# First six chunks' decays as sums of logarithms on TensorE, an explicit order of all tasks, and fillers on an on-chip tile

## The chip, the cores and the metric

One core of one Trainium2 chip runs the whole program. The metric is the device time of one execution in microseconds (us); lower is better. Engines: PE is TensorE (PEld its weight loads), DVE is VectorE, ACT is ScalarE, POOL is GpSimd, SP issues the DMAs.

## What is computed

Gated linear attention with a decay per channel, and behind it an RWKV channel mix. B=4, H=8, S=768, D=48; the mix has d_model 384 and d_ff 1024.

```python
f = 1 / (1 + exp(-f_logit))
for t in range(S):                       # per batch and head
    state = f[t][:, None] * state + outer(k[t], v[t])
    x[t] = q[t] @ state
x_prev = x shifted by one step
xk = mu_k * x + (1 - mu_k) * x_prev ;  xr = mu_r * x + (1 - mu_r) * x_prev
out = sigmoid(xr @ w_r) * (relu(xk @ w_k) ** 2 @ w_v)
```

The weights w_k, w_r, w_v come as 64-bit words.

## The kernel before

The sequence is cut into 24 chunks of 128 steps (6 for each batch entry) and into 8 units of three chunks. A chunk holds all eight heads as four pairs, 128 channels by 4x128 steps.

**Attention of chunk i** (`add_attention`). SP loads qk{i}, v{i} and, for a unit, the gate logits f{u}; ScalarE takes their sigmoid (`sf`, L469, L475). `b`: VectorE's scan multiplies the gates up along time into PSUM (L293). `ln`, `rb`: ScalarE makes 1/b as exp(-ln b) (L299, L301). `q`: q times b (L303); `kr`: GpSimd's k times 1/b (L311, L312); `n`, `k`: one Newton step for that reciprocal on VectorE (L323; L315, L319), which leaves k with its sign turned. `TR`: four TensorE transposes of k (L363); `kt`: their copy. `SP`: scores (L378) and state sums (L398). `m` masks the scores (for chunk 0 by ScalarE and GpSimd), `g`, `za`, `zb`, `T` carry the state. `YA`, `YB`: outputs from the state and from the chunk itself (L415), with `w` between them; `y` copies them to x (L447, scale -1).

**The mix of unit u** (`add_mix`). When y of its three chunks is there, six small DMAs spread rows of x (`sp`, L505). Then `d`, `xm` (L517 or L527; L530, L535), a split into a high part `xh` (L543, L544) and a low part `xl` (L550, GpSimd), and the products on TensorE, all at L558: 8 times `F` (9 matmuls each, with w_k), 3 times `R` (9 each, w_r), 6 times `W` (12 each, w_v): 171 matmuls of 128x384 for a unit. Between F and W stand relu `r`, squares `h` and `kk`, and their difference `l` (L596, GpSimd).

**Weights** (`add_words`). 18 pieces (4 of w_r, 8 of w_k, 6 of w_v) are loaded as words and turned into two parts each: `S`, `T`, `X` on VectorE (L676, L685, L688), `H` on ScalarE (L691), `L` on GpSimd (L695). F{u}.f needs piece f of w_k, R all of w_r, W{u}.t0 pieces 0 to 2 of w_v and W{u}.t1 pieces 3 to 5. Later 15 checks `cm` read the words once more (L745).

**Order.** `Plan.schedule` lists the tasks one after the other: among those that are ready it takes the one that starts earliest by its own estimates, with the table `PLACE` to decide between near ones; `emit` pins that order on every engine, so each engine works strictly down its list. A task with two ways (say `l` on GpSimd or VectorE) takes the one that would be done first. Where the list has TensorE waiting before the first F, fillers (L753: 128x64 matmuls of the loaded identity, in fours, not before 14 us and not before `cst` has landed) are put in. ScalarE begins with the sigmoid table, and `ex` (L768) changes to the table of exp and ln after the gates of units 0 and 1; the gates of unit 2 change there and back (L475, L477).

Of the kernel before, what the change touches and what calls it, by code (L numbers as in the profile page):

```python
# [111 lines left out]

class Plan:

    def __init__(self):
# [879 lines left out]
```

## Time and profile before

| | |
|---|---|
| three runs | median 353.2 us (352.62 to 354.17) |
| profiled execution | 352.86 us, span of the trace 350.7 us |
| busy | PE 318.9, DVE 248.7, ACT 213.3, POOL 195.1 us |
| first and last matmul of a mix | 50.82 us, 345.06 us |
| unit 0's first F to unit 1's first F | 50.82 to 92.29 us |

In the trace times count from the start of the span. A row of the timeline has start, duration, engine, line, operation, what is written and read, and in brackets the idle time before it with what ended it. "L558 PE" is all of the mix's matmuls.

### The profile page before, as it was taken

What the parts mean: (1) busy time and instruction counts of PE and PEld (TensorE: products, weight loads), DVE (VectorE), ACT (ScalarE), POOL (GpSimd) and SP (SyncE); (2) the same over time, 40 slices, a digit from 0 to 9 for tenths busy, and PEclk for the clock granted to TensorE, in tenths of its full rate; (3) what the DMA queues carried; (4) which work ended last, traced back from release to release, by engine and by line L of the source; (5) the groups of instructions that cost most, each with busy time, mean ns of one, the idle gap of its engine ahead of it and who ended that gap; (6) DMA issues with size and microseconds to landing.
All of it is one profiled execution on the core that took longest, in us unless ns stands there. A gap on an engine that the chain in (4) does not pass through costs nothing.

```text
span 350.7 us, 10802 instructions
## 1 busy us (share of the span) xinstructions
PE 318.9 (91%) x4450; PEld 304.2 (87%) x4450; DVE 248.7 (71%) x489; ACT 213.3 (61%) x437; POOL 195.1 (56%) x235
## 2 busy tenths in 40 slices
PE   0078799899999999999999999999999999999993
PEld 0067589788999999999999999999999999999993
DVE  7987899989989699758975689549963943913110
ACT  2785678777686818873686558582876156705520
POOL 2554588987687177715784268526880634814400
PEclk9998859999999999999999999999999999999999
DMA  8999252335741674638323352042401100010001
GB/s 270 406 359 377 88 195 97 120 105 178 242 126 38 223 251 123 218 117 286 124 83 121 118 194 86 3 122 68 137 10 41 48 27 19 1 47 22 1 26 52
DMA packets 20650, 45.32 MB, mean 129 GB/s; under 512 B 2928, under 2 KB 13040, under 8 KB 20592
## 3 DMA queue, kind: packets, MB, share of 16 engines
q1 hardware_dynamic: 20592, 44.55, 38.3%
q8 instruction: 37, 0.61, 0.7%
q14 instruction: 21, 0.17, 0.2%
HBM read 38.64 MB, written 4.72 MB: 124 GB/s over the span
## 4 chain that ended last, share of the span: by engine, by line
PE 78%; POOL 6%; DVE 4%; DMA 3%; ACT 3%; issue 3%; SPq 1%; DVEq 0%; POOLq 0%
PE pm L558 61%; PE py L415 7%; PE pss L378 3%; PE pm L363 3%; DMA f<-in_zt 2%; PE pss L398 2%; POOL k2l L596 2%; POOL wv L695 2%; POOL wk L695 1%; DMA words<-in_wv 1%; PE py L753 1%; DVE xm L535 1%; DVE qk L319 1%; POOL qk L311 0%; SPq L682 0%
## 5 line engine op out<-in xcount | busy, mean ns | idle before, releaser
L558 PE MATMUL pm<-xh,wk 128*128 128x384 f32 x384 | 105.3, 345 | 1.1 <-POOL wk L695 1.0
L558 PE MATMUL pm<-wv,k2h 128*128 128x384 f32 x384 | 98.9, 338 | 0.3 <-POOL wv L695 0.3
L596 POOL TENSOR_TENSOR k2l<-kk,k2h 128x384 fp32r<-128x384 f32 x64 | 68.3, 1069 | 36.5 <-DVE kk L588 25.3
L550 POOL TENSOR_TENSOR xl<-xm,xh 128x384 fp32r<-128x384 f32 x48 | 50.1, 1053 | 49.8 <-DVE xh L544 24.6
L558 PEld LDWEIGHTS pm<-xh,wk 128*128 128x128 f32 x384 | 70.1, 189 | 3.3 <-POOL wk L695 1.9
L558 PEld LDWEIGHTS pm<-wv,k2h 128*128 128x128 f32 x384 | 68.8, 188 | 0.8 <-POOL wv L695 0.6
L558 PE MATMUL pm<-xl,wk 128*128 128x384 f32 x192 | 64.8, 337 | 0.0
L558 PE MATMUL pm<-wv,k2l 128*128 128x384 f32 x192 | 64.5, 336 | 0.0
L581 ACT ACTIVATE r<-pm 128x384 f32<-128x384 f32 x56 | 27.5, 491 | 25.1 <-PE pm L558 23.7
L558 PE MATMUL pm<-wr,xh 128*128 128x384 f32 x144 | 37.9, 345 | 0.4 <-DVE kk L588 0.4
L586 ACT ACTIVATE k2h<-r 128x384 fp32r<-128x384 f32 x64 | 33.5, 525 | 5.6 <-DVE r L582 3.6
L648 DVE TENSOR_TENSOR o<-pm,lg 128x384 f32<-128x384 f32 x24 | 13.3, 553 | 33.0 <-PE pm L558 33.0
L558 PEld LDWEIGHTS pm<-xl,wk 128*128 128x128 f32 x192 | 36.4, 189 | 0.0
L558 PEld LDWEIGHTS pm<-wv,k2l 128*128 128x128 f32 x192 | 36.1, 188 | 0.0
L363 PE MATMUL pm<-ident,qk 128*128 128x128 f32 x96 | 17.1, 307 | 20.4 <-DVE qk L319 19.8
L588 DVE SCALAR_TENSOR_TENSOR kk<-pm,r 128x384 f32<-128x384 f32 x34 | 18.9, 555 | 22.4 <-ACT r L581 21.6
L293 DVE TENSOR_TENSOR_SCAN pm<-f,low 128x512 f32<-128x512 f32 x24 | 33.7, 1404 | 0.3 <-ACT ktk L367 0.2
L447 ACT ACTIVATE x<-py 64x128 f32<-64x128 f32 (+1 forms) x69 | 21.4, 310 | 19.9 <-PE py L415 18.2
L363 PEld LDWEIGHTS pm<-ident,qk 128*128 128x128 f32 x96 | 12.5, 154 | 21.9 <-DVE qk L319 19.6
L415 PEld LDWEIGHTS py<-qk,z 64*64 64x64 f32 x704 | 17.0, 141 | 11.9 <-issue 5.2
L415 PE MATMUL py<-qk,z 64*64 64x64 f32 x704 | 23.4, 236 | 4.0 <-ACT stage L447 1.4
L535 DVE SCALAR_TENSOR_TENSOR xm<-pm,mu_sb,x 128x384 f32<-128x384 f32 x42 | 25.7, 612 | 0.7
(102 smaller groups left out, 570.9 us busy)
## 6 DMA issues: line engine op xcount, KB each, us to landing
qk<-in_qkt SPq DMA_DIRECT2D x24, 512.0 KB, 4.3
words<-in_wv SPq DMA_DIRECT2D x12, 512.0 KB, 4.3
f<-in_zt SPq DMA_DIRECT2D x7, 768.0 KB, 6.4
v<-in_vt SPq DMA_DIRECT2D x24, 192.0 KB, 3.3
out<-o SPq DMA_DIRECT2D x24, 192.0 KB, 2.4
words<-in_wk SPq DMA_DIRECT2D x6, 512.0 KB, 4.6
words_k2h<-in_wk SPq DMA_DIRECT2D x4, 384.0 KB, 6.0
words_k2l<-in_wk SPq DMA_DIRECT2D x4, 384.0 KB, 8.4
```

The costliest lines, as they stand in the source:

```text
L293: pl.add(f"b{i}", ga, ("V", 1.25, 1, lambda: nc.vector.tensor_tensor_scan(b().rearrange(FL), f().rearrange(FL), self.low.rearrange(FL), 1. ...
L363: nc.tensor.transpose(pk()[:, j], k()[:, j], self.ident)
L415: first[c, h] = nc.tensor.matmul(to, lhs, rhs, start=(c, h) not in first, stop=stop, skip_group_check=True)
L447: e.activation(o, i_, AF.Copy, scale=-1.0)
L535: pl.add(f"xm{u}.{n}{j}", pr, ("V", 0.62, 0, lambda xm=xm, n=n, j=j: nc.vector.scalar_tensor_tensor(xm(), pm("d", u, j)[:, :UT], self.mu_s ...
L550: e.tensor_tensor(lo(), xm(), hi().bitcast(F32), op=ALU.subtract)
L558: nc.tensor.matmul(ps, lhs(a, j), rhs(bb, j), start=ends[0] and i == 0, stop=ends[1] and i == len(pr) - 1)
L581: pl.add(f"r{u}.{f}", kf, ("A", 0.5, 0, lambda r=r, ps=ps: nc.scalar.activation(r(), ps(), AF.Relu)), ("V", 0.56, 0, lambda r=r, ps=ps: nc ...
L586: pl.add(f"h{u}.{f}", kf, ("A", 0.53, 0, lambda r=r, hi=hi: nc.scalar.activation(hi(), r(), AF.Square)), after=[f"r{u}.{f}"], **kw)
L588: pl.add(f"kk{u}.{f}", kf, ("V", 0.56, 0, lambda r=r, ps=ps, kk=kk: nc.vector.scalar_tensor_tensor(kk(), ps(), 0.0, r(), op0=ALU.max, op1= ...
L596: e.tensor_tensor(lo(), kk(), hi().bitcast(F32), op=ALU.subtract)
L648: pl.add(f"o{u}.{t}", kv, ("V", 0.56, 0, lambda t=t, ps=ps, o=o: nc.vector.tensor_tensor(o(), ps(), lg()[:, t], op=ALU.mult)), after=[f"W{ ...
```

## The change

- For chunks 0 to 5 (`early`, units 0 and 1) the decays are made another way. VectorE clamps the gate logits in place (`sf`, now a maximum with a per-partition bound); TensorE transposes them (`zT`, 4 transposes), ScalarE takes exp and ln(1+.) of the transposes (`ez`, `ln`), TensorE multiplies with a triangle of ones (`b`, 4 matmuls of 128x128), which gives the sums of logarithms along time, and ScalarE's `rb` and `e` take exp of plus and minus that sum. The scan, `n`, `k` and `g` of these chunks are gone, and so is the sigmoid of units 0 and 1; y's sign is +1 there, and za multiplies with bl of the chunk before.
- ScalarE begins with the table of exp and ln; `ex` is gone. The triangle is one more load (`tri`).
- `ORDER` names every task in turn, and the engine where there are two; `schedule` follows it. Of 112 tasks `l` and `xl`, all on GpSimd before, 32 stand on VectorE.
- A filler is one matmul of 256 columns on `low`, a tile that a memset makes; it may come from 3.6 us on. There are 10 of them (20 before). `py` is cleared whole.

```diff
-FILL = (14.0, 0.85)
+FILL = (3.6, 0.9)
...
-PLACE = {
-    "cst": 0.45, "ex": 7.598, "c0": 0.906, "cm0": -1.376, "c2": -1.069, "v0": -3.667, "b0": 0.122, "bl0": -1.422, "rb0": 0.016,
...
+ORDER = """
+wr2 wrS2 f0.0 wrT2 sf0.0 wrX2 wr3 cst f0.1 wv0 tri f1 zT0 wrS3 wrT3 wrH2 sf0.1 wrX3 wvS0 wvT0 wvX0 sf1 ez0 ln0 zT1 wrH3 ez1
...
+        given = [t.partition(":")[::2] for t in reversed(ORDER.split())]
...
+            if given:
+                n, e = given.pop()
...
+        if early:
+            def sums_of_logs():
+                for j in range(NP):
+                    nc.tensor.matmul(b()[:, j], f()[:, j], self.tri, start=True, stop=True)
...
+            def over_time():
+                for j in range(NP):
+                    nc.tensor.transpose(zt()[:, j], f()[:, j], self.ident)
...
+            pl.add(f"ez{i}", ga, ("A", 0.63, 0, lambda: nc.scalar.activation(f(), zt(), AF.Exp, scale=-1.0)),
+                   uses=[("pm", ("z", i))])
+            pl.add(f"ln{i}", ga, ("A", 0.63, 0, lambda: nc.scalar.activation(f(), f(), AF.Ln, bias=1.0)), after=I("ez"))
...
+            pl.add(f"rb{i}", ga, ("A", 0.63, 0, lambda: nc.scalar.activation(rb(), b(), AF.Exp)),
+                   takes=[("rb", i)], uses=[("pm", ("b", i))])
+            pl.add(f"e{i}", ga, ("A", 0.63, 0, lambda: nc.scalar.activation(b(), b(), AF.Exp, scale=-1.0)),
...
-            pl.add(f"g{i}", ga, ("G", 0.25, 0, lambda: gate(nc.gpsimd)),
+            if not early:
+                pl.add(f"g{i}", ga, ("G", 0.25, 0, lambda: gate(nc.gpsimd)),
...
+        def sure(cs=slice(0, UC)):
+            nc.vector.tensor_scalar(t(cs), t(cs), self.sure, None, op0=ALU.max)
...
-            self.nc.tensor.matmul(self.py[:, 0, 256:320], self.ident, self.ident[:, :64], start=False, stop=True, skip_group_check=True)
+            self.nc.tensor.matmul(self.py[:, 0, 256:], self.low[:, 0], self.low[:, 1:3], start=False, stop=True, skip_group_check=True)
...
-    nc.scalar.preload_act_table_set(SIGMOID_SET)
+    nc.scalar.preload_act_table_set(EXP_SET)
...
-    nc.vector.memset(k.py[:, :, :320], 0.0)
+    nc.vector.memset(k.py[:, :, :], 0.0)
```

How the order moves, at the head of three engines. First VectorE before, just behind the pieces of w_r (pm are PSUM buffers, f the gates, low the scan's lower bound, bl the last column of b, rb its reciprocal):

```order
L688 SCALAR_TENSOR_TENSOR lg0_119<-lg0_119,pm3_94 128x288
L293 SCALAR_TENSOR_TENSOR pm0_91<-f0_61,low_78 128x512
L297 COPY bl_80<-pm0_91 128x4
L293 SCALAR_TENSOR_TENSOR pm1_92<-f0_61,low_78 128x512
L297 COPY bl_80<-pm1_92 128x4
L293 SCALAR_TENSOR_TENSOR pm2_93<-f0_61,low_78 128x512
L303 TENSOR_TENSOR qk1_65<-qk1_65,pm1_92 128x512
L293 SCALAR_TENSOR_TENSOR pm3_94<-f1_62,low_78 128x512
```

And VectorE in the change, from the first clamp on (L517 is the clamp; L730, L739, L742 are S, T, X of a piece of weights, x0 and lg0 of w_r, words0 of w_v, words_k2h of w_k; L350 is q):

```order
L517 TENSOR_SCALAR f0_61<-f0_61,sure_70 128x512
L742 SCALAR_TENSOR_TENSOR x0_106<-x0_106,pm2_95 128x288
L730 TENSOR_SCALAR pm3_96<-words0_122 128x512
L739 SCALAR_TENSOR_TENSOR pm3_96<-words0_122,pm3_96 128x512
L742 SCALAR_TENSOR_TENSOR words0_122<-words0_122,pm3_96 128x512
L517 TENSOR_SCALAR f1_62<-f1_62,sure_70 128x1536
L350 TENSOR_TENSOR qk0_64<-qk0_64,pm2_95 128x512
L348 COPY bl_82<-pm2_95 128x4
L730 TENSOR_SCALAR pm2_95<-words_k2h0_131 128x384
L739 SCALAR_TENSOR_TENSOR pm2_95<-words_k2h0_131,pm2_95 128x384
```

The scans are gone from VectorE's list, and pieces of w_v and w_k stand in their place. TensorE before, its first rows (L363 transposes k, L378 and L398 are SP, L753 a filler, L415 an output):

```order
L363 MATMUL pm0_91<-ident_68,qk0_64 128x128 x4
L363 MATMUL pm1_92<-ident_68,qk1_65 128x128 x4
L378 MATMUL pss_87<-qk0_64 64x64 x16
L398 MATMUL pss_87<-v0_101,ktk0_99 48x48 x16
L753 MATMUL py_88<-ident_68 128x64 x4
L415 MATMUL py_88<-qk0_64,z01_73 64x64 x4
```

And in the change (L807 is a filler, L327 zT, L321 b, L413 TR):

```order
L807 MATMUL py_90<-low_80 128x256
L327 MATMUL pm1_94<-ident_68,f0_61 128x128 x4
L807 MATMUL py_90<-low_80 128x256
L327 MATMUL pm0_93<-ident_68,f0_61 128x128 x4
L321 MATMUL pm2_95<-tri_69,f0_61 128x128 x4
L321 MATMUL pm1_94<-tri_69,f0_61 128x128 x4
L327 MATMUL pm0_93<-ident_68,f1_62 128x128 x4
L327 MATMUL pm3_96<-ident_68,f1_62 128x128 x4
L807 MATMUL py_90<-low_80 128x256 x2
L413 MATMUL pm0_93<-ident_68,qk0_64 128x128 x4
```

Fillers and the gates' transposes and sums stand ahead of the first TR now. ScalarE before, from its first sigmoid of unit 1 on (L299 and L301 are ln and rb):

```order
L475 ACTIVATE f1_62<-f1_62 128x1536
L768 ACT_TABLE_LOAD
L299 ACTIVATE rb0_95<-pm0_91 128x512
L301 ACTIVATE rb0_95<-rb0_95 128x512
L299 ACTIVATE rb1_96<-pm1_92 128x512
L301 ACTIVATE rb1_96<-rb1_96 128x512
```

And in the change (L330 ez, L332 ln, L334 rb, L336 e):

```order
L330 ACTIVATE f0_61<-pm1_94 128x512
L332 ACTIVATE f0_61<-f0_61 128x512
L745 CAST wr0_85<-x0_106 128x288
L330 ACTIVATE f0_61<-pm0_93 128x512
L332 ACTIVATE f0_61<-f0_61 128x512
L334 ACTIVATE rb0_97<-pm2_95 128x512
L336 ACTIVATE pm2_95<-pm2_95 128x512
```

The table change between gates and ln is gone, and a chunk has four passes of 128x512 where it had two beside its sigmoid.

## Rows read from the trace of the kernel before

**Rows 1.** The page's second part: PE's busy tenths in 40 slices of the span.

```profile
PE   0078799899999999999999999999999999999993
```

**Rows 2.** Stretches: start:end, length, then busy us (and count) of each engine.

```profile
0.00:50.80 50.80, 26.42 (x712) 23.16 (x712) 43.06 (x92) 32.73 (x65) 26.03 (x44) 0.88 0.80 284
50.80:92.30 41.50, 39.85 (x384) 36.60 (x381) 37.97 (x68) 30.31 (x65) 34.55 (x35) 0.98 0.47 147
92.30:131.20 38.90, 38.90 (x637) 37.51 (x636) 33.13 (x61) 25.34 (x53) 24.34 (x31) 1.00 0.52 162
```

**Rows 3.** The chain that ended last, its start: start, us, what.

```profile
5.05 7.82 DMA f<-in_zt
12.89 1.48 ACT f L475
14.39 1.28 ACT L768
```

**Rows 4.** The same chain: the first F's of units 2 and 3.

```profile
131.42 3.13 PE pm L558 x18
...
168.96 3.18 PE pm L558 x18
```

**Rows 5.** Timeline of TensorE from 110 to 115 us: one chunk's steps between matmuls of R.

```profile
110.16 0.60 PE L363 MATMUL pm<-ident,qk 128*128 128x128 f32 x4
110.52 0.60 PE L558 MATMUL pm<-wr,xh 128*128 128x384 f32 x2
...
112.26 0.46 PE L415 MATMUL py<-qk,z 64*64 64x64 f32 x16
112.54 0.65 PE L378 MATMUL pss<-qk 64*64 64x64 f32 x32
...
114.17 0.62 PE L558 MATMUL pm<-wr,xh 128*128 128x384 f32 x2
```

**Rows 6.** VectorE's groups from 0 to 92.3 us: count | busy us, mean ns.

```profile
L293 DVE TENSOR_TENSOR_SCAN pm<-f,low 128x512 f32<-128x512 f32 x9 | 12.0, 1337 | 0.1
L323 DVE TENSOR_TENSOR pm<-rb,pm 128x512 f32<-128x512 f32 x8 | 5.5, 691 | 0.3 <-ACT rb L301 0.3
L319 DVE SCALAR_TENSOR_TENSOR qk<-pm,qk 128x128 f32<-128x128 f32 x16 | 3.8, 281 | 0.0
L315 DVE SCALAR_TENSOR_TENSOR qk<-pm,qk 128x256 f32<-128x256 f32 x8 | 3.3, 418 | 0.7 <-DVE pm L323 0.5
L685 DVE SCALAR_TENSOR_TENSOR pm<-words,pm 128x512 int32<-128x512 int32 x6 | 4.2, 692 | 0.1
L685 DVE SCALAR_TENSOR_TENSOR pm<-words_k2h,pm 128x384 int32<-128x384 int32 x4 | 2.2, 562 | 0.1
L544 DVE CAST xh<-xm 128x384 fp32r<-128x384 f32 x5 | 1.9, 390 | 0.2
```

**Rows 7.** ScalarE's passes of 128x512 over the whole span: count | busy us, mean ns.

```profile
L301 ACT ACTIVATE rb<-rb 128x512 f32<-128x512 f32 x24 | 15.0, 626 | 0.4
```

**Rows 8.** Timeline, the end of unit 0's y (ACT) to its first F.

```profile
37.48 0.98 ACT L447 ACTIVATE x<-py 128x256 f32<-128x256 f32 x3 [1.15 <-PE py L415]
...
50.82 0.69 PE L558 MATMUL pm<-xh,wk 128*128 128x384 f32 x1
```

**Rows 9.** Timeline of TensorE: the same filler at two places.

```profile
45.97 1.81 PE L753 MATMUL py<-ident 128*128 128x64 f32 x8
54.69 1.00 PE L753 MATMUL py<-ident 128*128 128x64 f32 x8
```

**Rows 10.** GpSimd's groups from 50.8 to 92.3 us.

```profile
L695 POOL TENSOR_TENSOR wv<-words,wv 128x512 fp32r<-128x512 f32 x6 | 9.9, 1643 | 1.5 <-ACT wv L691 1.5
L695 POOL TENSOR_TENSOR wk<-words_k2l,wk 128x384 fp32r<-128x384 f32 x4 | 4.2, 1046 | 1.1 <-ACT wk L691 1.1
```

**Rows 11.** Timeline, two scans, the first with GpSimd at work beside it.

```profile
12.19 1.57 DVE L293 TENSOR_TENSOR_SCAN pm<-f,low 128x512 f32<-128x512 f32 x1
14.41 1.23 DVE L293 TENSOR_TENSOR_SCAN pm<-f,low 128x512 f32<-128x512 f32 x1
```

More of the change, by code (lines that the diff above doesn't have):

```diff
@@ L27 @@
 NF = DFF // P
-SIGMOID_SET = "sigmoid_and_others"
 EXP_SET = "natural_log_exp_and_others"
@@ L31 @@
 N, U = B * NCH, B * NU
+NL = 2
+SURE, FULL = -44.0, 40.0
 NQ, NFB = 4, 3
@@ L160, in schedule @@
         order = []
+        given = [t.partition(":")[::2] for t in reversed(ORDER.split())]
         while ready:
             best = None
-            for n, names in ready.items():
+            if given:
+                n, e = given.pop()
+                _, _, ways, _, takes, _ = self.tasks[n]
+                way = next(w for w in ways if w[0] == e or not e)
+                at = max([0.0] + [min(slots[b[0]])[0] for b in takes]
+                         + [end[m] for m in ready[n] if way_of[m] != way[0]])
+                best = None, n, max(at, free[way[0]]), way
+            for n, names in ready.items() if best is None else ():
                 _, place, ways, _, takes, _ = self.tasks[n]
@@ L180, in schedule @@
             e, us, port, _ = way
-            if e == "P" and self.filler and "cst" in end:
-                t = max(free["P"], read, FILL[0], end["cst"])
-                stop = t + (start - t - 0.25) * FILL[1]
+            if e == "P" and self.filler:
+                t = max(free["P"], read, FILL[0])
+                stop = t + (start - t - 0.15) * FILL[1]
                 cold = t + 6.0 if last_p == "F" else 0.0
-                while t + (us4 := 1.76 if t < cold else 0.88) < stop:
+                while t + (us4 := 0.9 if t < cold else 0.46) < stop:
                     name = f"fill{len(order)}"
-                    fw = "P", 0.88, 0, lambda: self.filler(4)
+                    fw = "P", 0.46, 0, lambda: self.filler(1)
                     self.tasks[name] = (name, 0.0, (fw,), (), (), ())
@@ L271, in add_attention @@
         cs = i % NCH
+        early = u < NL
         at = i / UC - LEAD
@@ L290, in add_attention @@
         rb = lambda: self.b("rb", i)
-        pl.add(f"b{i}", ga, ("V", 1.25, 1, lambda: nc.vector.tensor_tensor_scan(
-            b().rearrange(FL), f().rearrange(FL), self.low.rearrange(FL), 1.0, op0=ALU.mult, op1=ALU.max)),
-            after=[f"sf{u}.{c}" if u == 0 else f"sf{u}"], takes=[("pm", ("b", i))])
+        sf = f"sf{u}.{c}" if u == 0 else f"sf{u}"
+        if early:
+            def sums_of_logs():
+                for j in range(NP):
+                    nc.tensor.matmul(b()[:, j], f()[:, j], self.tri, start=True, stop=True)
+            zt = lambda: self.b("pm", ("z", i)).rearrange("p (a c) -> p a c", a=NP)
+            def over_time():
+                for j in range(NP):
+                    nc.tensor.transpose(zt()[:, j], f()[:, j], self.ident)
+            pl.add(f"zT{i}", ga, ("P", 0.45, 0, over_time), after=[sf, "cst"], takes=[("pm", ("z", i))])
+            pl.add(f"ez{i}", ga, ("A", 0.63, 0, lambda: nc.scalar.activation(f(), zt(), AF.Exp, scale=-1.0)),
+                   uses=[("pm", ("z", i))])
+            pl.add(f"ln{i}", ga, ("A", 0.63, 0, lambda: nc.scalar.activation(f(), f(), AF.Ln, bias=1.0)), after=I("ez"))
+            pl.add(f"b{i}", ga, ("P", 1.2, 0, sums_of_logs), after=I("ln") + ["tri"], takes=[("pm", ("b", i))])
+            pl.add(f"rb{i}", ga, ("A", 0.63, 0, lambda: nc.scalar.activation(rb(), b(), AF.Exp)),
+                   takes=[("rb", i)], uses=[("pm", ("b", i))])
+            pl.add(f"e{i}", ga, ("A", 0.63, 0, lambda: nc.scalar.activation(b(), b(), AF.Exp, scale=-1.0)),
+                   after=I("rb"), uses=[("pm", ("b", i))])
+        else:
+            pl.add(f"b{i}", ga, ("V", 1.25, 1, lambda: nc.vector.tensor_tensor_scan(
+                b().rearrange(FL), f().rearrange(FL), self.low.rearrange(FL), 1.0, op0=ALU.mult, op1=ALU.max)),
+                after=[sf], takes=[("pm", ("b", i))])
+            pl.add(f"ln{i}", ga, ("A", 0.63, 0, lambda: nc.scalar.activation(rb(), b(), AF.Ln)),
+                   takes=[("rb", i)], uses=[("pm", ("b", i))])
+            pl.add(f"rb{i}", ga, ("A", 0.63, 0, lambda: nc.scalar.activation(rb(), rb(), AF.Exp, scale=-1.0)),
+                   after=I("ln"), uses=[("rb", i)])
@@ L296, in add_attention @@
+        whole = I("e" if early else "b")
         pl.add(f"bl{i}", ga, ("A", 0.2, 0, lambda: nc.scalar.copy(self.bl[:, i], b()[:, :, C - 1])),
                ("V", 0.15, 0, lambda: nc.vector.tensor_copy(self.bl[:, i], b()[:, :, C - 1])),
-               uses=[("pm", ("b", i))])
-        pl.add(f"ln{i}", ga, ("A", 0.63, 0, lambda: nc.scalar.activation(rb(), b(), AF.Ln)),
-               after=["ex"], takes=[("rb", i)], uses=[("pm", ("b", i))])
-        pl.add(f"rb{i}", ga, ("A", 0.63, 0, lambda: nc.scalar.activation(rb(), rb(), AF.Exp, scale=-1.0)),
-               after=I("ln"), uses=[("rb", i)])
+               after=whole, uses=[("pm", ("b", i))])
@@ L303, in add_attention @@
         pl.add(f"q{i}", ga, ("V", 0.69, 0, lambda: nc.vector.tensor_tensor(q(), q(), b(), op=ALU.mult)),
-               after=I("qk"), uses=[("pm", ("b", i))])
+               after=whole + I("qk"), uses=[("pm", ("b", i))])
         def halves(t):
@@ L365, in add_attention @@
         kt_in = lambda: pk().rearrange("p a (r c) -> p a r c", r=2)[:, :, :, :D]
-        pl.add(f"TR{i}", at, ("P", 0.44, 0, tr), after=I("k") + ["cst"], takes=[("pm", ("k", i))])
+        pl.add(f"TR{i}", at, ("P", 0.44, 0, tr), after=I("kr" if early else "k") + ["cst"], takes=[("pm", ("k", i))])
         pl.add(f"kt{i}", at, ("A", 0.5, 0, lambda: nc.scalar.copy(self.b("ktk", i), kt_in())),
@@ L446, in y_out @@
                 if e is nc.scalar:
-                    e.activation(o, i_, AF.Copy, scale=-1.0)
+                    e.activation(o, i_, AF.Copy, scale=sign)
                 else:
-                    e.tensor_scalar(o, i_, -1.0, None, op0=ALU.mult)
-        pl.add(f"y{i}", at, ("A", 1.2, 0, lambda: y_out(nc.scalar)), ("V", 1.2, 0, lambda: y_out(nc.vector)),
+                    e.tensor_scalar(o, i_, sign, None, op0=ALU.mult)
+        sign = 1.0 if early else -1.0
+        pl.add(f"y{i}", at, ("A", 1.27, 0, lambda: y_out(nc.scalar)), ("V", 1.35, 0, lambda: y_out(nc.vector)),
                after=I("YB"), **({"takes" if c == 0 else "uses": [("x", u), ("stage", u)]}))
@@ L457, in add_unit @@
         gates = [f"{n}{i}" for i in range(UC * (u - NFB), UC * (u - NFB + 1)) for n in "bg"
-                 if i >= 0 and (n == "b" or i % NCH > 0)]
+                 if i >= 0 and (n == "b" or i % NCH > 0 and i >= UC * NL)]
         ga = u - LEAD - GATE
@@ L468, in add_unit @@
                 pl.add(f"f0.{c}", ga - 0.4, ("Q", 0.71, 1, lambda cs=cs: load(cs)))
-                pl.add(f"sf0.{c}", ga - 0.4, ("A", 0.63, 0, lambda cs=cs: nc.scalar.activation(t(cs), t(cs), AF.Sigmoid)),
-                       after=[f"f0.{c}"] + ([f"sf0.{c - 1}"] if c else []))
+                pl.add(f"sf0.{c}", ga - 0.4, ("V", 0.43, 1, lambda cs=cs: sure(cs)), after=[f"f0.{c}"])
+        elif u < NL:
+            pl.add(f"f{u}", -1.5 + 0.1 * u, ("Q", 2.13, 1, load))
+            pl.add(f"sf{u}", -1.3 + 0.1 * u, ("V", 0.96, 1, sure), after=[f"f{u}"])
         else:
@@ L475, in sf @@
                     nc.scalar.activation(t(), t(), AF.Sigmoid)
-                    if SPLIT and u == 2:
-                        nc.scalar.preload_act_table_set(EXP_SET)
-                pl.add(f"sf{u}", -1.0 if SPLIT and u == 2 else -9, ("A", 1.5 + 2.6 * (SPLIT and u == 2), 0, sf),
-                       after=[f"f{u}", ("ex" if SPLIT else "sf1") if u > 1 else "sf0.2"])
+                    nc.scalar.preload_act_table_set(EXP_SET)
+                pl.add(f"sf{u}", -1.0, ("A", 4.1, 0, sf), after=[f"f{u}", f"sf{u - 1}"])
             else:
@@ L526, in add_mix @@
                 if halved:
-                    pl.add(f"d{u}.{n}{j}", pr, ("A", 0.5, 0, lambda n=n, j=j: nc.scalar.activation(
+                    pl.add(f"d{u}.{n}{j}", pr, ("A", 0.59, 0, lambda n=n, j=j: nc.scalar.activation(
                         pm("d", u, n, j)[:, :UT], x()[:, j, 1:], AF.Copy, scale=self.mu_sb[:, n, j : j + 1])),
@@ L628, in add_mix @@
         pl.add(f"sg{u}", k0 + 0.45, ("A", 2.5 + (1.3 if u < U - 1 else 0) + (1.48 if more else 0), 0, sig),
-               after=[f"lg{u}.{t}" for t in range(UC)] + ([f"f{u + NFB}"] if more else []) + (["ex"] if not alone else []),
+               after=[f"lg{u}.{t}" for t in range(UC)] + ([f"f{u + NFB}"] if more else []),
                uses=[("lg", u)])
@@ L690, in piece @@
                 after=[f"{name}T{p}"], uses=[t_key, home])
-            pl.add(f"{name}H{p}", place, ("A", us(0.00104, 0.12), 0, lambda: nc.scalar.copy(hi(), x())),
+            pl.add(f"{name}H{p}", place, ("A", us(0.00104, 0.14), 0, lambda: nc.scalar.copy(hi(), x())),
                    after=[f"{name}X{p}"], uses=[home])
@@ L767, in add_start @@
                 self.one_mu, self.mu_sb, -1.0, 1.0, op0=ALU.mult, op1=ALU.add)), after=["mu"])
-        pl.add("ex", -9, ("A", 1.3, 0, lambda: nc.scalar.preload_act_table_set(EXP_SET)),
-               after=["sf1" if SPLIT else f"sf{NFB - 1}"])
+        pl.add("tri", -1.9, ("Q", 0.18, 1, lambda: nc.sync.dma_start(self.tri, self.cst[:, 1])))
         lo = lambda: self.b("xm", "lo")[:, 0:2]
@@ L862, in rwkv_kernel @@
     }
-    nc.scalar.preload_act_table_set(SIGMOID_SET)
+    nc.scalar.preload_act_table_set(EXP_SET)
+    nc.vector.memset(k.sure, FULL)
+    for r in (0, 64):
+        nc.vector.memset(k.sure[r : r + D], SURE)
     nc.vector.memset(k.low, LOW)
     nc.vector.memset(k.low[:, :, 0:1], 1.0)
-    nc.vector.memset(k.py[:, :, :320], 0.0)
+    nc.vector.memset(k.py[:, :, :], 0.0)
     nc.vector.memset(k.pss[:, :, 256 : 256 + NP * D], 0.0)
```

84 lines of the change are left out of this document (75 added, 9 removed), and 51 rows, old and new, of the table PLACE.

## The prediction, made before the change was run

> **What bounds the kernel now.** I read the page first. PE's slices read 9 tenths or more from the ninth on; what is open is the beginning [rows 1]. The stretches cut that beginning at unit 0's first F (50.8 us) and unit 1's first F (92.3 us) [rows 2]. Up to 50.8 us PE works 26.4 us, and VectorE 43.1; from 50.8 to 92.3 VectorE is at 37.97 of 41.5 us (91.5%), GpSimd at 34.55; from 92.3 us on PE has no gap (38.90 of 38.90). So VectorE sets the pace of the first 92 us and TensorE that of the rest, and a microsecond gained ahead of 92.3 us arrives at the end if PE then stays full. The profiled execution took 352.86 us (span 350.7), 0.1% under the median of 353.2; the sum is made against 352.86. A measurement of this kernel can tell about 0.5% (1.8 us) from no change.
>
> What a unit costs TensorE when it never waits: 18 matmuls take 3.13 us, 0.174 each, so 171 take 29.7; units 2 and 3 begin 37.54 us apart [rows 4], which leaves 7.8 us for three chunks of attention, 2.6 each with the changes between the two kinds. One chunk's steps are TR 0.36 (110.16 to 110.52), YA 0.28, SP and YB together 1.63 (112.54 to 114.17) [rows 5]. I split the 1.63 in halves and scale to 2.6: TR 0.4, SP 0.95, Y 1.25.
>
> The head's chain waits 7.82 us for the gates, then passes the sigmoid of unit 1 (1.48) and the table change (1.28) before the first ln can start at 15.7 us [rows 3]. In the change that pair is gone.
>
> **Part 1: VectorE up to unit 0's first F.** At 50.8 us the kernel before has behind it six scans, n's and k's, and 4 pieces of w_r, 2 of w_k, 1 of w_v. The change has none of these scans, n's and k's (chunk 6's scan stands there), but 4, 7 and 3 pieces. Removed: six times 1.34 + 0.69 + 0.42 + 2 x 0.28 = 3.01, so 18.1 us [rows 6]; two copies kt go to ScalarE, some 1.1. Added: one scan, 1.3; five pieces of w_k at three passes of 0.56 and two of w_v at three of 0.69, 8.4 + 4.1 [rows 6]; the longer memset of py, 0.3; the clamps. The trace has no clamp of 128x512: a cast of 128x384 took 0.39, so at least 0.52 in proportion, and a pass over 128x512 words 0.69 [rows 6]; I take 0.55, nearest the cast, which like the clamp has one fp32 input on chip, and 1.6 for the 1536 wide one: 3 x 0.55 + 1.6 = 3.2. The Trainium skill ("VectorE: DVE Perf Modes", section "The perf-mode tier table (the rule you actually need)") gives such an operation on fp32 the double rate, 1227 ns at 2048 elements; by it the clamps would cost some 1 us less, an estimate. Net: -18.1 - 1.1 + 1.3 + 12.5 + 0.3 + 3.2 = -1.9. So 41.2 us of work; with the same idle time as before (50.8 - 43.1 = 7.7) the first F comes at 48.9. I take 49.5, since ScalarE is fuller there too: for six chunks it gains two passes of 0.63, 7.6 us [rows 7], and loses unit 0's three sigmoids of as many columns, unit 1's of 1.48 and a table load of 1.28 [rows 3], 4.7 in all.
>
> The lower bound is the chain without any wait: the third y's first three copies end at 38.46 in the kernel before, and F starts 12.4 us later [rows 8]. Following the new lists by the rows' durations, chunk 0's ln is ready near 7.8, its sum near 10.3, and the third y ends near 34, so F at 46 at the earliest, and VectorE's list without idle time gives 47.4. The upper bound is three more us of waits, 52.5.
>
> **Part 2: from F to F, unit 0 to unit 1.** Before, this takes 41.5 us and holds 171 matmuls (29.7), 2 TR, 1 SP and 1.75 Y (3.9): 7.9 us are lost. Part of the loss is three groups of fillers of 1.0 us, of which one stands there [rows 9]; the rest is late pieces: GpSimd's L passes for w_k and w_v alone are 16 us there, 9.9 for w_v and 4.2 for the k2l half of w_k [rows 10]. In the change no filler stands behind the first F, and four pieces of w_k, one of w_r, three of w_v are left, some 9.9 us. I scale what remains: (7.9 - 3.0) x 9.9 / 16 = 3.0, between the bounds 0 and 7.9. The change's list holds more attention there: 3 TR, 3 SP, 2.75 Y (7.5). So 29.7 + 7.5 + 3.0 = 40.2, and unit 1's first F comes at 89.7, 2.6 us before the old one. By then 1 TR, 2 SP and 1 Y more are done than before, 0.4 + 1.9 + 1.25 = 3.5 us that TensorE need not do later.
>
> **Part 3: the rest.** Nothing is added for TensorE behind 92 us: its matmuls are the same, it has six changes fewer between mix and attention (73 for 79), which I leave out, and the last o and its DMA stand as before. Twelve groups of transposes and sums and ten fillers lie in the head, covered by waits, if that cover holds. What could spoil it is VectorE: 32 of the 112 passes l and xl come to it. In unit 1 its list adds up to 34.8 us by the rows' durations; up to 92.3 us the durations of all its groups add up to 87 where the busy time is 81.0 [rows 2], so some 32.4 busy. At the 91.5% seen there that needs 35.4 us and TensorE 37.5, so it is hidden; at the 85% of 92.3 to 131.2 us [rows 2] 38.1, 0.6 more. Later units have 2 to 5 us less on VectorE. I count 0.
>
> Sum: 352.9 - 2.6 - 3.5 = **346.8 us** (1.7% faster).
>
> **The rivals.**
> *TensorE becomes the bound of the head.* The same filler took 1.81 us for its eight records at 46 us and 1.00 at 54.7 [rows 9]: the pace of the clock's lower and upper level (1.2 and 2.4 GHz); the stretch before 50.8 was granted 0.88 on average, the next 0.98 [rows 2]. The change adds six zT and six b ahead of F, and only ten fillers, too few to keep the engine working through its waits. At the slow pace (0.226 a record) zT costs 1.1, b 1.9 (its four matmuls make 8 records, as the filler's four do), a filler of 256 columns 0.85, TR 1.1, and SP and Y twice the above, 1.9 and 2.5: 6.6 + 11.4 + 8.5 + 6.6 + 11.4 + 11.9 = 56.4 us from 5.3 on, so F at 61.7 without any wait. Then 61.7 + 40.2 - 3.5 = 98.4 against 92.3: 359.0, slower. It decides from F at 55.6 on. For it: the head before 50.8 shows such slow stretches. Against it: PE has far more to do there now, and at the upper level the sum is half, 28 us. Chance 0.09.
> *ScalarE and VectorE, both nearly full, wait for each other* along the fixed lists: the head's idle time on VectorE grows from 7.7 to 11 us and part 2 loses 5.5: F at 52.5, next F at 95.2, less 3.5: 352.3, no change. For it: ez, ln, rb and e stand one behind the other ahead of every q. Against it: pieces of weights stand between, ready to fill. Chance 0.12.
> *VectorE and GpSimd hold each other up.* A scan took 1.57 with GpSimd at work beside it and 1.23 without [rows 11]. Passes with both inputs on chip, which l and xl are, come to VectorE 8 times up to unit 2. At 0.34 each that is 2.7 us, inside the slack of part 3; a whole GpSimd pass of 1.05 each [rows 10] is 8.4, of which 2 are hidden: 353.2. The Trainium skill ("SBUF — State Buffer", section "Who interferes with whom") has the two engines share one pair of ports under an exclusive lock, so that the later one waits for the whole instruction. The trace differs: the scan lost a third of a GpSimd pass [rows 11]. Chance 0.04.
> *The order does less than it says*: the first F moves but part 2 keeps its 7.9 us: 351.7, inside no change, within the second rival's chance.
>
> **How the numbers follow.** Forecast 0.75, between its bounds: 47.4 and no loss give 29.7 + 7.5 + 47.4 = 84.6, so 341.7; 52.5 and 5.5 give the second rival. TensorE's case is 0.09, the exchange of waits 0.12, the ports 0.04. The range from 342.5 to 352.3 leaves out the best corner and the slow cases, about 0.2. Faster by over 0.5% 0.75, within 0.5% 0.15 (the second rival and most of the third), slower 0.10.
>
> **What would show it.** Right: unit 0's first F at 48 to 51 us, unit 1's at 87 to 92, no PE gap behind it; VectorE over 85% busy up to there, without scans before 40 us; ScalarE's first ln near 8 us. Wrong: PE without gaps ahead of 50 us at the lower clock; idle PE behind 95 us that VectorE ends; a first F later than 53 us; or GpSimd passes of twice their length beside VectorE's l.

## The result and the profile after

The changed kernel takes 349.27 us in the median of four runs (347.78 to 351.27), the kernel before 353.69 beside it: a ratio of 0.987, 95% interval 0.984 to 0.991. That is 1.3% faster; forecast were 346.8 us and a range of 342.5 to 352.3. The profiled execution took 349.33 us, its span is 347.5 us. Ratios here are of fast runs alone: they leave out one run of e6, which took 351.96 us at a granted clock of 0.976 where the others of e6 had 0.991 to 0.996.

The page's second part, PE's slices and the granted clock, which answer to [rows 1]:

```profile
PE   4877959999999999999999999999999999999993
PEclk9998787999999999999999999999999999999999
```

TensorE is at work from the first slice on, and full from the seventh. Two stretches at the lower clock lie in the head (the granted clock is 0.50 from 34 to 38 us and from 49.05 to 55.88 us).

The stretches, cut at the new first F's of units 0, 1 and 2, against [rows 2]:

```profile
0.00:52.40 52.40, 37.65 (x789) 30.39 (x789) 41.12 (x89) 36.97 (x80) 26.44 (x40) 0.90 0.86 300
52.40:93.00 40.60, 39.88 (x556) 37.87 (x552) 36.50 (x65) 30.14 (x65) 31.15 (x35) 0.96 0.37 118
93.00:130.20 37.20, 37.20 (x557) 36.15 (x552) 31.30 (x67) 25.00 (x56) 17.43 (x22) 1.00 0.41 139
```

VectorE (third number behind the length) worked 41.12 us up to the first F, where the forecast had 41.2; but it idled 11.3 us in that stretch, 7.7 in the kernel before. What VectorE waited for up to the first F, after and then before (engine, line, releaser: us, times, longest):

```profile
DVE z L399 <- PE pss L448: 2.6, 2, 1.4
DVE f L517 <- DMA f<-in_zt: 2.2, 2, 1.2
DVE qk L350 <- ACT bl L347: 1.5, 1, 1.5
...
DVE pm L730 <- DMA words<-in_wv: 0.7, 1, 0.7
DVE pm L730 <- DMA words_k2h<-in_wk: 0.6, 1, 0.6
DVE pm L730 <- DMA x<-in_wr: 0.5, 1, 0.5
...
DVE qk L350 <- DMA qk<-in_qkt: 0.4, 1, 0.4
DVE pm L730 <- DMA words_k2l<-in_wk: 0.3, 1, 0.3
```

```profile
DVE pm L676 <- DMA x<-in_wr: 1.1, 1, 1.1
```

Loads made it wait 4.7 us instead of 1.1: without scans it reaches its pieces sooner than they land. A q stood 1.5 us behind a copy bl on ScalarE.

The timeline of TensorE: the first F of unit 0, that of unit 1, the last matmul; then the last matmul of the kernel before.

```profile
52.38 0.69 PE L612 MATMUL pm<-xh,wk 128*128 128x384 f32 x1
...
93.00 0.45 PE L612 MATMUL pm<-xh,wk 128*128 128x384 f32 x1
...
341.63 0.34 PE L612 MATMUL pm<-wv,k2l 128*128 128x384 f32 x1
```

```profile
344.72 0.34 PE L558 MATMUL pm<-wv,k2l 128*128 128x384 f32 x1
```

From unit 1's first F to the end of the last matmul it is 249.0 us (93.00 to 341.97), where the kernel before needed 345.06 - 92.29 = 252.8. So the change gains 3.8 us behind that F, and has lost 0.7 us when it gets there.

### The profile page after: what moved, and what is told of

The parts are those of the page before. It is cut to its first block, busy times and chain, and to the rows that moved or that the text cites. A ratio compares the mean times of both kernels' runs of the same rounds, so it can differ in the third digit from the quotient of the medians.

```text
span 347.5 us, 10849 instructions
## 1 busy us (share of the span) xinstructions
PE 325.9 (94%) x4502; PEld 310.1 (89%) x4502; DVE 250.7 (72%) x512; ACT 210.5 (61%) x441; POOL 152.0 (44%) x187
## 4 chain that ended last, share of the span: by engine, by line
PE 83%; DVE 5%; ACT 5%; DMA 2%; SPq 1%; issue 1%; POOL 0%; DVEq 0%; ACTq 0%
PE pm L612 68%; PE py L465 7%; PE pss L428 3%; PE pm L413 3%; DMA words_k2h<-in_wk 2%; PE pss L448 2%; DVE pm L730 1%; DVE pm L739 1%; PE pm L321 1%; ACT wk L745 1%; ACT x L497 1%; DVE qk L350 1%; ACT pm L581 1%; ACT kk L644 0%; SPq L514 0%
## 5 line engine op out<-in xcount | busy, mean ns | idle before, releaser
L650 POOL TENSOR_TENSOR k2l<-kk,k2h 128x384 fp32r<-128x384 f32 x43 | 45.1, 1054 | 65.6 <-ACT k2h L640 28.4
L612 PEld LDWEIGHTS pm<-wv,k2h 128*128 128x128 f32 x384 | 68.5, 188 | 0.8
L604 POOL TENSOR_TENSOR xl<-xm,xh 128x384 fp32r<-128x384 f32 x37 | 40.6, 1103 | 53.7 <-DVE xh L598 21.1
L635 ACT ACTIVATE r<-pm 128x384 f32<-128x384 f32 x51 | 24.7, 488 | 27.7 <-PE pm L612 26.7
L640 ACT ACTIVATE k2h<-r 128x384 fp32r<-128x384 f32 x64 | 32.3, 519 | 14.0 <-DVE r L636 13.5
L612 PE MATMUL pm<-wr,xh 128*128 128x384 f32 x144 | 36.8, 337 | 0.7 <-DVE words L742 0.7
L358 POOL TENSOR_TENSOR qk<-qk,rb 128x256 f32<-128x256 f32 x20 | 15.8, 791 | 34.5 <-ACT rb L344 16.2
L612 PEld LDWEIGHTS pm<-wr,xh 128*128 128x128 f32 x144 | 25.9, 188 | 1.0 <-DVE words L742 1.0
L465 PEld LDWEIGHTS py<-qk,z 64*64 64x64 f32 x704 | 16.2, 139 | 11.9 <-issue 4.8
L339 DVE TENSOR_TENSOR_SCAN pm<-f,low 128x512 f32<-128x512 f32 x18 | 26.5, 1471 | 0.3
L465 PE MATMUL py<-qk,z 64*64 64x64 f32 x704 | 22.3, 234 | 4.2 <-ACT done L484 3.5
L612 PE MATMUL pm<-wr,xl 128*128 128x384 f32 x72 | 24.2, 336 | 0.0
```

What stands on the lines that cost most here:

```text
L339: pl.add(f"b{i}", ga, ("V", 1.25, 1, lambda: nc.vector.tensor_tensor_scan(b().rearrange(FL), f().rearrange(FL), self.low.rearrange(FL), 1. ...
L358: e.tensor_tensor(k()[:, ::2], k()[:, ::2], rb()[:, ::2], op=ALU.mult)
L465: first[c, h] = nc.tensor.matmul(to, lhs, rhs, start=(c, h) not in first, stop=stop, skip_group_check=True)
L604: e.tensor_tensor(lo(), xm(), hi().bitcast(F32), op=ALU.subtract)
L612: nc.tensor.matmul(ps, lhs(a, j), rhs(bb, j), start=ends[0] and i == 0, stop=ends[1] and i == len(pr) - 1)
L635: pl.add(f"r{u}.{f}", kf, ("A", 0.5, 0, lambda r=r, ps=ps: nc.scalar.activation(r(), ps(), AF.Relu)), ("V", 0.56, 0, lambda r=r, ps=ps: nc ...
```

## The experiments

Unless said otherwise, a run keeps the buffers, the fillers and every engine's list of the changed kernel but for the tokens shown; a token is a step of the order, and b, ln, q and bl of one chunk touch one PSUM buffer. The runs write the ten fillers into the order as tokens `_`. Each measured ratio is to the kernel before, run beside it. Line numbers in the rows of e1 to e6, e9 and e10 are 6 higher than in the changed kernel (F is L618, ln of chunk 6 L348, its scan L345).

**e1, three waits of the head.**

```diff
-e3 bl2:A y1:A ... q2
+e3 q2 bl2:A y1:A ...
-wvS1 ... m3 onemu wkT5
+onemu wvS1 ... m3 wkT5
-YA4 xm0.01 xh0.01:V m4 T4 bl5:V xh0.02:A d0.10 xm0.10 w4:A kt5:A
+YA4 m4 xm0.01 xh0.01:V T4 bl5:V w4:A kt5:A xh0.02:A d0.10 xm0.10
```

> The changed kernel with three waits of the head taken out of its fixed order: q of chunk 2 is recorded ahead of the copy bl of the same chunk on ScalarE (VectorE stood 1.49 us before that q at 29.2 us, released by bl, though it needs only e); the small pass one_mu stands at 36 us, where GpSimd is idle, and not at 42.8 us (1.03 us there for a pass that took 0.16 in the kernel before); and m of chunk 4 and the copies w and kt ahead of YB4 stand two places earlier (TensorE stood 1.84 us at 49.7 us). Buffers and fillers are those of the changed kernel. Theory (waits that the fixed order holds put unit 0's first F at 52.4 us instead of the 49.5 forecast, and behind unit 0 only TensorE counts): of 1.5 + 0.9 + 1.2 = 3.6 us on that chain two to three arrive, first F at 49.5 to 50.5 us, 346.5 to 347.5 us. Rival (such waits are absorbed by the next wait, since DMA arrivals or TensorE's own pace set the head): first F at 52 us or later, 349 to 349.5 us.

Measured: 349.16 us, ratio to before 0.989 (0.984 to 0.994): no change against the changed kernel. Its timeline, the two first F's:

```profile
49.26 0.44 PE L618 MATMUL pm<-xh,wk 128*128 128x384 f32 x1
...
92.83 0.45 PE L618 MATMUL pm<-xh,wk 128*128 128x384 f32 x1
```

The first F came 3.1 us earlier than in the first profile (2.0 earlier than in e12's), as the theory had it, and unit 1's F stayed. What the engines waited for between 46 and 57 us, and the chain there (start, us, what):

```profile
PE pm L618 <- ACT r L641: 2.9, 1, 2.9
```

```profile
ACT rb L348 <- DVE qk L356: 4.3, 1, 4.3
```

```profile
45.84 8.26 DMA qk<-in_qkt
54.10 0.02 issue
54.12 0.70 DVE qk L356
...
54.91 0.60 ACT rb L348
55.50 0.39 ACT r L641
```

ln of chunk 6 (L348) needs only the scan, which ended at 51.3 us. It waited for q of chunk 6, which reads the same PSUM buffer and was recorded first; q came late behind three passes of a piece of w_k on VectorE's list, and then waited 0.4 us for its load. Behind ln stands r of unit 0, and F0.2 needs its buffer. Both theories had half: the waits were real, and the next one took the gain.

**e5, the same with two reads recorded the other way round.** No engine's own list changes.

```diff
-q6 wvS2 wvT2 wvX2 ln6
+ln6 q6 wvS2 wvT2 wvX2
-ln7 rb7 w6:A kr7:G bl7:V
+bl7:V ln7 rb7 w6:A kr7:G
```

> The kernel of e1_waits with two more changes of the recorded order: ln of chunk 6 (ScalarE) ahead of q of chunk 6 (VectorE), and bl of chunk 7 (VectorE) ahead of ln of chunk 7 (ScalarE). Each engine's own list stays as it is; only which of two readers of one PSUM buffer is recorded first changes. In e1_waits the first F came at 49.26 us as the forecast had it, but ScalarE then stood 4.25 us (released by q of chunk 6, which waited for its load until 54.1 us) and TensorE 2.90 us behind it. Theory (a read recorded second waits for the read recorded first, on whichever engine, and so the gain of e1_waits was handed to the next such wait): ScalarE's gap of 4.25 shrinks to below 1, TensorE's 2.90 to below 0.5 and its 0.71 at 72.3 goes, unit 1's first F at 89 to 90.5 us, 345.5 to 347 us. Rival (unit 0 is bound by its loads and by GpSimd's pieces of the weights, whichever wait stands first): the gap moves to TR6, R or W, unit 1's first F at 92 us or later, 348.5 to 349.5 us.

Measured: 346.07 us, ratio 0.981 (0.975 to 0.986). ScalarE's waits between 46 and 58 us and unit 1's first F:

```profile
ACT bl L353 <- DVE qk L356: 1.0, 1, 1.0
ACT rb L348 <- DVE pm L345: 0.5, 1, 0.5
```

```profile
89.53 0.45 PE L618 MATMUL pm<-xh,wk 128*128 128x384 f32 x1
```

The 4.3 us are 0.5, now behind the scan; both gaps of TensorE behind the first F (2.9 us, and 0.7 at 72.3) are gone; unit 1's F comes 3.3 us earlier though the first F of this profile came only at 50.7. The theory holds. But two reads were turned at once, and no run turns one alone. An estimate from the rows of this run: ln of chunk 7 ended here at 68.5 us, the scan before it at 66.25, so that with ln6 turned alone the copy bl of chunk 7 and the conversion behind it would have come 2.3 us later, and TensorE, which needed that conversion's buffer at 68.9 and had it at 68.6, would have stood some 2 us. By this estimate the larger part of the 3.3 us is the second read's.

**e6, the load of chunk 6 earlier.**

```diff
-wk7 qk7 wv2 f3 qk6
+qk6 wk7 qk7 wv2 f3
```

> The kernel of e5_reads with the load of q and k of chunk 6 three places earlier on the queue, ahead of a piece of w_k, of the load for chunk 7 (which waits for YB3), of a piece of w_v and of unit 3's gates. Theory: if in e5_reads the load of chunk 6 is still what comes late (its landing at 54 us ends a wait of VectorE or, over k and TR6, of TensorE), it lands some 4 us earlier and another 0.5 to 1.5 us come: 345 to 346 us. Rival (the load is hidden once the two reads stand the other way round): same as e5_reads within 0.7 us.

Measured: 345.33 us, ratio 0.974 (0.968 to 0.979); first F's at 49.69 and 89.11 us, the second 0.4 earlier than in e5. The two do not tell the theories apart: once ln no longer waits for q, the load matters little or not at all.

**e12, the changed kernel again.**

> The changed kernel once more, on the chip and beside the runs of the three kernels above: 348.5 to 350 us, first F at 52 to 53 us and unit 1's first F at 93 us; the distance from unit 1's first F to the last matmul 249.0 us, as in e1 to e7.

Measured: 349.26 us, ratio 0.987 (0.983 to 0.992). Its first F's, the stretch around the first (clock third from the end), TensorE's wait there, and ScalarE's row of ln; below, ScalarE's same row in the first profile of this kernel:

```profile
51.23 0.44 PE L612 MATMUL pm<-xh,wk 128*128 128x384 f32 x1
...
92.87 0.45 PE L612 MATMUL pm<-xh,wk 128*128 128x384 f32 x1
```

```profile
50.00:55.00 5.00, 5.00 (x130) 4.59 (x120) 4.93 (x11) 2.64 (x8) 5.00 (x7) 1.00 0.97 377
```

```profile
PE pm L612 <- ACT r L635: 1.6, 1, 1.6
```

```profile
55.57 0.60 ACT L342 ACTIVATE rb<-pm 128x512 f32<-128x512 f32 x1 [2.87 <-DVE qk L350]
```

```profile
55.54 0.60 ACT L342 ACTIVATE rb<-pm 128x512 f32<-128x512 f32 x1 [2.85 <-DVE qk L350]
```

This was not planned as a test of the clock, and is one. In the first profile the clock was granted at half (its lower level, 1.2 GHz) from 49.05 to 55.88 us, and the first 18 matmuls of F took 4.99 us. Here it was at the upper level and they were done earlier; then TensorE waited 1.6 us for the same ln at the same time. First F's at 49.26, 51.23 and 52.38 us (e1, e12, the first profile) all lead to 92.8 to 93.0: the first F did not set the second.

In the first profile TensorE never waited for that ln; what the three share stands later. TensorE's second group of R (R0.1) in the first profile, in e12 and in e1, and the copy bl of chunk 7 on VectorE in the first profile:

```profile
72.51 0.44 PE L612 MATMUL pm<-wr,xh 128*128 128x384 f32 x1 [0.72 <-DVE words L742]
```

```profile
72.39 0.45 PE L612 MATMUL pm<-wr,xh 128*128 128x384 f32 x1 [1.60 <-DVE words L742]
```

```profile
72.34 0.44 PE L618 MATMUL pm<-wr,xh 128*128 128x384 f32 x1 [0.71 <-DVE words L748]
```

```profile
70.17 0.16 DVE L348 COPY bl<-pm 128x4 f32<-128x4 f32 x1 [1.47 <-ACT rb L342]
```

R0.1 takes the PSUM buffer of a piece of w_v, whose conversion VectorE begins behind that bl; and bl, which needs only the scan, waited for ln of chunk 7 on ScalarE, recorded first: 1.47 us here, 2.29 in e12, 1.95 in e1. From R0.1 to unit 1's first F it is 20.5 us in all three. This is the second read that e5 turned round.

**e2, fillers into the gaps ahead of the first F.**

```diff
-YB3 ... SP4 ... TR5 YA4 ... YB4
+YB3 ... _ _ SP4 ... _ TR5 YA4 ... _ _ _ _ YB4
```

> The changed kernel with seven more fillers on TensorE (two ahead of SP4, one ahead of TR5, four ahead of YB4), all in gaps that it has between 43.7 and 49.7 us. Theory of the clock (the granted clock stood at its lower level from 49.05 to 55.88 us because PE waited 3.9 of the 6 us before): PE stays at the upper level, unit 0's first 18 matmuls take 3.2 us instead of 4.99, 347.5 to 348 us. Rival (the waits of the fixed order set the first F, and the clock costs nothing further on because late l and xl cover it): first F unchanged at 52.4 us, the next unit's first F unchanged at 93 us, 349 to 349.5 us. If the fillers come in the way of SP4, TR5 or YB4: up to 1 us later.

Measured: 352.63 us, ratio 0.997 (0.994 to 0.999); first F's at 55.10 and 95.34 us. TensorE's waits between 43 and 53 us:

```profile
PE py L813 <- ACT stage L503: 3.6, 1, 3.6
PE py L813 <- ACT done L490: 0.8, 1, 0.8
```

The fillers write the tile from which y is read, and waited for that read themselves. They came in the way, more than the 1 us allowed for, and the run says nothing on the clock.

**e3, unit 1's gates later on the queue.**

```diff
-tri f1 ... wvX0 sf1 ez0 ... qk0 wk0 ... zT5 zT4 ... ez5 ... ez4 ... ln4 ln5
+tri ... qk0 wk0 f1 ... wkX0 sf1 ... kt0:V zT5 zT4 ez5 ez4 ln4 ln5
```

> The changed kernel with unit 1's gate load (768 KB) behind the first piece of w_k on the queue, its clamp behind that piece's conversion, and the transposes, exps and logarithms of chunks 4 and 5 moved behind it. VectorE waited for DMA arrivals for 4.4 us in the first 15 us (1.21 of it for this load), 1.1 us in the kernel before. Theory of the arrivals (they make the difference in idle time between 7.7 us forecast and 11.3 us measured, and they are passed on): VectorE has 1 to 2 us of conversions done earlier, first F at 50.5 to 51.5 us, 347.5 to 348.5 us. Rival (they are absorbed by the later waits for SP and for ScalarE): first F at 52 to 52.5 us, 349 to 349.5 us; with chunks 4 and 5 late it could be 350.

Measured: 350.68 us, ratio 0.992 (0.989 to 0.994); first F's at 53.26 and 94.17 us. Some buffers of the head change places with it. VectorE waited 1.48 us for the same load at 16.2 us instead. Moving one load behind another moved the wait, and unit 1's first F came 1.2 us later than in the first profile.

**e10, the mask's two loads later**, on top of e6.

```diff
-cst(ident, mask, mask) f0.1 wv0 tri f1 qk0 wk0 ... v0
+cst(ident) f0.1 wv0 tri f1 qk0 wk0 ... v0 mask(mask, mask)
```

> The kernel of e6_load with the two small loads of the mask, which stand fifth and sixth on the queue and take 1.2 us of it, behind the load v of chunk 0 (the mask is first read at 22 us). Theory of the arrivals (VectorE waits some 5 us for loads in its first 16, and the queue issues them one behind the other): the loads behind it are issued 1.2 us earlier, VectorE idles about 1 us less, first F near 48.7 us, 344 to 345 us. Rival (the DMA engines are full from 10 us on and the next loads come as late as before): first F as in e6_load, 345 to 345.7 us.

Measured: 343.62 us, ratio 0.973 (0.969 to 0.977). Waits of VectorE in the first 16 us, in e6 and in e10:

```profile
DVE f L523 <- DMA f<-in_zt: 1.8, 2, 1.1
DVE pm L736 <- DMA words<-in_wv: 1.2, 1, 1.2
...
DVE pm L736 <- DMA words_k2h<-in_wk: 0.8, 1, 0.8
```

```profile
DVE f L523 <- DMA f<-in_zt: 1.1, 1, 1.1
...
DVE pm L736 <- DMA words<-in_wv: 0.7, 1, 0.7
...
DVE pm L736 <- DMA words_k2h<-in_wk: 0.3, 1, 0.3
```

First F's at 47.55 and 86.98 us, both 2.1 earlier than in e6, twice what was expected. The medians differ by 1.7 us, though single runs overlap. Arrivals are passed on to the end when all loads come sooner; the queue's order of issue was part of it.

**e9, two more waits**, on top of e10: `wkL1:G` behind `xl0.00:G`, `w0:A` ahead of `wkH2 ln3`.

> The kernel of e10_mask with two more moves of the order: GpSimd's pass for a piece of w_k (wkL1) behind the first xl of unit 0 instead of ahead of it (in e6_load the cast xh of VectorE took 1.16 us instead of 0.35, to the end of that GpSimd pass), and the copy w of chunk 0 ahead of a piece's copy and of an ln on ScalarE (TensorE stood 1.70 us at 24.4 us, released by it). Theory (every wait of the head that lies on its chain arrives at the end, as unit 1's first F sets it): 0.8 and 0.5 us on top of e10_mask, 342.5 to 344 us. Rival (the next wait takes them): as e10_mask within 0.7 us.

Measured: **343.25 us**, ratio 0.971 (0.968 to 0.974), the fastest of the study, 6.0 us under e12 beside it. First F's at 47.12 and 86.55 us. Against e10 that is 0.4 us: TensorE's wait for the copy w fell from 1.71 to 0.75 us, and YB0 then waited 0.84 us for GpSimd's mask pass. The rival holds. With both reads turned the second F does follow the first: from the one to the other it is 39.4 us in e6, e10 and e9, whose first F's lie up to 2.6 us apart.

**e4, all l and xl on GpSimd:** every `:V` of these tokens is `:G`.

> The changed kernel with all 112 passes l and xl on GpSimd (32 of them are on VectorE). Theory (behind unit 0 only TensorE counts, VectorE and GpSimd are hidden): unit 0's part of it, two passes of 1.05 us on a GpSimd that is busy 31 of 40.6 us there, may make its W late by up to 1 us; later units nothing; 349 to 350.5 us. Rival (the split keeps TensorE fed, or the waits of VectorE for GpSimd's instructions count): GpSimd gets 34 us more, l comes late to W in several units, over 352 us; or the stalls of VectorE vanish and the time falls by 1 us or more.

Measured: 350.68 us, ratio 0.991 (0.987 to 0.995). Unit 1's first F came at 93.80, 0.8 to 0.9 late, from there 249.0 us as before. The time lies 0.2 us above the range of the theory. The split of 32 passes is worth about a microsecond in unit 0 and nothing behind it.

**e7, the decays undone, the order kept.** Scans, n, k and sigmoids are those of the kernel before.

> The kernel before, with its scans, but in the order of the changed kernel: the decays of chunks 0 to 5 are undone (six scans, n's and k's are back on VectorE, the sigmoids of units 0 and 1 on ScalarE), everything else keeps its place in the fixed order, where it is ready; eight of the ten fillers stay. Theory (the change pays because VectorE has 18 us less to do in the head, which the order fills with pieces of weights and more attention): VectorE gets 18 us more in a head in which it idles 11.3 us of 52.4, of which some absorb it; first F at 60 to 68 us, 357 to 366 us. Rival (the order alone makes the gain, the decays are hidden): first F below 56 us, 349 to 353 us.

Measured: 370.13 us, ratio 1.047 (1.041 to 1.052). First F at 72.06 us; the stretch up to it:

```profile
0.00:72.00 72.00, 31.32 (x712) 26.04 (x712) 53.21 (x111) 34.47 (x72) 30.93 (x50) 0.86 0.65 224
```

The 12 us that VectorE works more push the first F back by 19.7: later than either theory said. The fixed order now waits at places made for other durations: between 46 and 120 us TensorE waits 7.6 us for q and 6.2 us for the copy ktk. From unit 1's first F (112.98 us) to the last matmul it is 249.0 us here too.

**e8, the decays kept, the order left to the planner:** `ORDER = ""`.

> The changed kernel without its explicit order: the planner with its small table of places sets it, fillers as the planner puts them. Theory (the decays free VectorE, but the gain comes only if pieces of weights and attention are drawn into the freed time): somewhere between before and after plus a few us, 350 to 358 us, with TensorE gaps behind unit 0. Rival (the order adds nothing, the decays do it all): 348.5 to 350 us.

Measured: 363.47 us, ratio 1.028 (1.022 to 1.033); first F at 58.87 us, the next at 98.92, and 256.3 us from there. Both theories missed: the time lies above the two ranges. Each half of the change alone is slower than the kernel before, for which a long table of places had been fitted; the short table here had not been fitted to stand alone.

**e11, no fillers:** the ten tokens `_` are left out.

> The changed kernel without its ten fillers, all else in place. Theory (they lie in waits and matter little, since TensorE's pace does not set the head): the granted clock is at its lower level longer in the first 50 us, first F 52.4 to 54 us, 349 to 350.5 us. Rival (they hold the clock up in the head, where transposes and sums are on the chain): first F at 55 us or later, 352 us or more. Beside it: TensorE stood 0.3 to 2.4 us inside SP2 in seven kernels, always at its record 347, released by nothing that the trace shows, with the loads at full rate. If that belongs to the place in the program, it comes at the same record again, now 14 records further on in the work; if to SP2, at the same step.

Measured: 350.29 us, ratio 0.991 (0.988 to 0.994), 1.0 us over e12 beside it, though single runs overlap (349.59 to 351.70, and 348.26 to 350.47); first F's at 53.27 and 94.52 us; granted clock from 16 to 50 us 0.82, in e12 0.90. The theory holds. The stall inside SP2 did not come, neither at the record nor at the step.

## Why the prediction was right and wrong

The direction held. The gain was too large: 6.1 us were forecast, the two profiled executions differ by 3.5 and the medians by 4.4. The loss lies ahead of unit 1's first F (93.0 us instead of 89.7). Of the signs named, ScalarE's first ln (7.24 us) and the first scan (51.19 us) stood where they should; both first F's, 52.4 and 93.0 us, missed the marks of 48 to 51 and 87 to 92, and VectorE was 83% busy up to unit 1's first F, where over 85 was the mark.

*Part 1, the account of VectorE's work: right in its sum, partly by luck.* 41.2 us forecast, 41.12 measured. Inside it the clamps were too dear:

```profile
L517 DVE TENSOR_SCALAR f<-f,sure x4: 479/484/1020, 4.6 to 16.0; 128x512 f32<-128x512 f32 x3, 128x1536 f32<-128x1536 f32 x1
```

3 x 0.48 + 1.02 = 2.5 us instead of 3.2. The double rate that the Trainium skill ("VectorE: DVE Perf Modes", "The perf-mode tier table (the rule you actually need)") gives, about 1 us less by that estimate, was the better guide. Two terms that the sum lacked made up for it: one copy kt more than it counted stayed on VectorE (0.55 us), and one_mu took 1.03 us instead of 0.16.

*Part 1, "with the same idle time as before": wrong*, and this is the step that failed first. 11.3 us instead of 7.7 put the first F at 52.4 us, beyond the 49.5 taken and just inside the bound of 52.5. Work that leaves an in-order engine brings it sooner to everything it must wait for: 3.6 us more of loads and 1.5 us of a read recorded second came, while some waits of the kernel before went. e1 took that read and two other waits out and had its F at 49.26; from e6 to e10 earlier loads gave 2.1 us.

*Part 2, "from F to F" as a length of its own: wrong in form for this kernel, right in number by luck* (40.6 against 40.2). The sum added 29.7 + 7.5 + 3.0 to whatever the first F is, the 3.0 for late pieces. Of the 3.4 us lost in the first profile, 1.9 are the first 18 matmuls at the lower clock (4.99 us instead of 3.13) and 0.7 is the wait ahead of R0.1. e1, e12 and the first profile show three first F's up to 3.1 us apart and one second F. What held it were reads recorded second, places that the forecast never looked at: in all three bl of chunk 7 behind ln of chunk 7, and ahead of it, in e1 and e12, ln of chunk 6 behind q of chunk 6. So a first F at 49.5 would not have given 89.7. e5 shows the step that did: 89.5. How much each of the two reads cost is an estimate only. Once both are turned the form holds, at 39.4 us (e6, e10, e9).

*The attention moved ahead and part 3: right.* 3.5 us forecast, 3.8 measured, the six turns that were left out among them. Behind unit 1's first F TensorE has one gap of 0.5 us in the first profile, and 249.0 us pass from that F to the last matmul there and in e1 to e7 and e9 to e12; only e8, with another list, has another number. e7 has it without the decays, so these 3.8 us belong to the order. VectorE's 32 passes are hidden behind that F, as e4 shows.

*The rivals.* The head's wait for each other of ScalarE and VectorE (first F at 52.5) is what came, at its full size; its second half (5.5 us lost from F to F) did not, nor did a part 2 that keeps its 7.9: 3.4 were lost. TensorE at the lower clock came for 7 us and decided nothing: e12 had the upper level and the same second F. The lock of VectorE and GpSimd exists, and the forecast misread it. It said that a scan "lost a third of a GpSimd pass" [rows 11]. GpSimd has two passes beside its scans there, merged in one row of the kernel before, from 9.42 us on:

```profile
9.42 3.24 POOL L695 TENSOR_TENSOR wr<-lg,wr 128x288 fp32r<-128x288 f32 x2 [1.52 <-ACT wr L691]
```

They end at 12.66. The scan that [rows 11] shows first started at 12.19, while the second pass ran, and ended at 13.76, 1.10 us behind that pass. So the 0.34 us that it lost follow from what was left of the pass when it came (0.47 us), and are no fixed share of a pass. The Trainium skill ("SBUF — State Buffer", "Who interferes with whom") says just this, the later engine waits out the whole instruction, and the trace agrees. It did not cost what that rival priced, since behind unit 0 VectorE has time to spare.

## What to carry to other kernels

When work is taken off an engine with a fixed list, its idle time does not stay: follow the shortened list to the next load or foreign engine at each step, before the freed time is counted as gained. In an order written out by hand, of two readers of one PSUM buffer on two engines, record the one first that can run first; it costs nothing, and two such turns were worth some 3 us here. Ask of every stage mark whether the next mark follows from it, or from something else with a clock of its own, and test it by moving the first.
